# Fp32 idle matmuls, a score tile moved back and early roots behind the exponentials, at the start of an attention and MLP kernel

## The chip, the cores and the metric

One core of one Trainium2 chip. The metric is the device time of one execution in microseconds (us).

In the profile PE is TensorE (PEld its weight loads), ACT is ScalarE, DVE is VectorE, POOL is GpSimd and SP is the engine that issues most DMAs. L232 is line 232 of the kernel; the changed kernel has one line more ahead of most statements, so L231 before is L232 after.

## The reference

```python
# attention over 8 batches x 12 heads, 448 positions, 64 per head
q_n, k_n = rmsnorm(q, g_q), rmsnorm(k, g_k)
scores = (q_n @ k_n.T) / 8
attn = exp(scores - max(scores)); attn = attn / (sum(attn) + 1e-9)
x = (attn @ v)                          # to (3584, 768)
# MLP over the 3584 tokens
h = x @ w_in                            # 768 -> 2048
g = maximum(h, 0) + alpha * minimum(h, 0)
out = g @ w_out                         # 2048 -> 768
```

## The kernel before

The heads of a batch are taken in pairs, six groups a batch, 48 in all. Per group: squares of q and k (`sq`), row sums (`ss`, VectorE), the reciprocal root in two small ScalarE steps (`rr`), the scaled q and k (`qs`, GpSimd mostly), their transposes (`qT`, `kT`: for the first groups by TensorE, later by DMA, followed by a VectorE product with the gain), scores (`sc`, TensorE), the exponential (`expT`, ScalarE), the denominator (`dn`) and the values (`av`). The product of values and reciprocal denominator is `xT` (VectorE), which feeds the MLP: `hT` (TensorE), `ah` = alpha x hT (ScalarE), `gT` = max(hT, ah) (VectorE), and the output product `op` or `opa`, copied to `osb` by VectorE.

Work is written in bursts: some score tiles and their exponentials, then some MLP units to fill TensorE. In all timelines below an engine runs its own instructions in the order in which they are written. In batch 0 there is no MLP work yet; idle matmuls (`spin`) fill TensorE there.

```python
idle = gT[:, 0, :S]                      # zeros to multiply, in a row of gT
nc.vector.memset(idle, 0.0)
# ... (cut)
def begin(ft):                           # units 0 to 3 of batch 0 start before xT is whole
    if ft < 2:
        begun[ft] = bank("hT", False)
    elif ft == 2:                        # units 2 and 3: two banks of ONE tile, hTb
        t = psa.tile([128, 2, 512], FP32, name="hTb", tag="acc")
        begun[2], begun[3] = t[:, 0], t[:, 1]
    up_part(begun[ft], 0, ft, 0, G - 1)

def up(b, ft, spare=False):
    # ... (matmuls of the unit into hT)
    ah = ffn.tile([128, S], FP16, name="ah", tag="ah", bufs=3)
    nc.scalar.activation(out=ah, in_=hT[:, :S], func=AF.Copy, scale=alpha_sb[:, ft : ft + 1])
    nc.vector.tensor_max(out=gT[:, ft, ds((b & 1) * S, S)], in0=hT[:, :S], in1=ah)

def spin(count):
    if count:
        ps = psf.tile([128, 512], FP32, name="spin", tag="mm")
        for _ in range(count):
            nc.tensor.matmul(out=ps[:, :S], lhsT=ident, rhs=idle, start=True, stop=True)
# ... (cut)
spin(22)
ct = psf.tile([128, 512], FP32, name="ct", tag="mm")   # alpha and gains, transposed
nc.tensor.transpose(ct[:, : NF + 2], rows, ident32[: NF + 2, : NF + 2])
spin(6)
# ... (cut: main loop, burst n)
    if lead:                             # the burst of group 2's denominator
        begin(3)
        for t in tiles[2:]:
            score(*t)
    for t in tiles[:1] if wait else tiles[1:] if lead else first_tiles:
        soft(*t)
    # ... (cut)
    if n in roots:
        y = roots[n]
        work = [(root, (y,)), (scale, (y, "q")), (scale, (y, "k"))]
        if lead:
            late = [(3, f, a) for f, a in work]
        else:
            for f, a in work:
                f(*a)
    # ... (cut)
    if n < den_at[G - 1] - 1 and plain and n not in turns:
        spin(4)
```

## Time and profile before

| what | before |
|---|---|
| time, median of 3 runs | 435.9 us (435.75 to 436.28) |
| span of the profiled run | 434.5 us |
| PE busy / ACT / DVE / POOL | 96% / 64% / 47% / 40% |
| TensorE instructions as compiled (weight loads and matmuls) | 9986 |
| granted clock, mean | 0.995 (half for one window, 13.5 to 16.9 us) |

From 57 us on TensorE is the bound and its only large gap is one of 1.49 us ahead of 85.93, so only its gaps in the start can be won.

In the profile of the kernel before, the queue q8 (instruction) has 39 packets of 16 KB each (0.64 MB), beside 9986 TensorE instructions: one packet for 256 of them on average. The prediction and the text below call such a stretch of TensorE's instructions a block; that it is 256 long is an estimate from these two counts, and the two stalls at numbers 705 and 1729, 4 x 256 apart, agree with it.

Two further views matter for what came of it; they are not in the prediction. The first is ScalarE's timeline at the fourth `ah`, which reads the second bank of hTb. The second is VectorE's timeline at 90 us, around the DMA transpose of the k of group 7. Columns of a timeline: start, duration, engine, line, operation, output <- input, shape, count, and in brackets the idle time ahead of it and what ended it.

```profile
45.39 0.64 ACT L353 ACTIVATE ah<-hTb,cols 128x448 f16<-128x448 f32 x1
...
46.73 0.64 ACT L353 ACTIVATE ah<-hTb,cols 128x448 f16<-128x448 f32 x1 [0.24 <-DVE gT L354]
```
```profile
90.86 0.55 DVE L191 TENSOR_SCALAR kT<-kT,gain 128x896 f16<-128x896 f16 x1 [0.49 <-DMA kT<-qs]
91.73 1.09 DVE L311 TENSOR_TENSOR xT<-av,rden 128x896 f16<-128x896 f32 x1 [0.31 <-PE av L260]
92.73 2.07 DVE L153 TENSOR_REDUCE ss<-sq 128x14 f32<-128x896 f32 x2
94.72 0.55 DVE L376 COPY osb<-op 128x384 f32<-128x384 f32 x1
```

The reader is to see two waits that look harmless. The fourth `ah` waits for a `gT`, though its own hT is done; 0.24 us, because a root stood between. And VectorE goes from kT to osb almost without a gap: a delay of kT at 90.86 by more than the 0.31 us that xT still waits for av delays osb at 94.72.

### The profile page before, as it was taken

Reading aid. Unit: us, or ns where it says so; the run is one execution under the profiler, and the core shown is the slowest. Engines: PE = TensorE matmul, PEld = TensorE weight load, DVE = VectorE, ACT = ScalarE, POOL = GpSimd, SP = SyncE. Lnnn points to the kernel's source line nnn. Section 1 sums busy time; section 2 is a strip of 40 time slices with the busy share of each in tenths; the row PEclk is TensorE's granted clock in tenths of the full one; section 3 lists DMA queues with packets and bytes.
Section 4 is the critical chain, followed back from the end, with each engine's and each line's share of the span. In section 5 each row is a group of like instructions: output and inputs, shape, how many; then the busy total and the mean of one; then the engine's idle time right before and its main releaser. Section 6 shows DMA issues by size and latency. Waiting matters only on the chain.

```text
span 434.5 us, 11509 instructions
## 1 busy us (share of the span) xinstructions
PE 417.4 (96%) x4977; PEld 215.9 (50%) x4977; DVE 204.9 (47%) x304; ACT 279.4 (64%) x385; POOL 175.8 (40%) x133
## 2 busy tenths in 40 slices
PE   7888799899999999999999999999999999999996
PEld 3344344354455445544555445554555545555564
DVE  3755564544554463546454463555453354233421
ACT  4997787588877577758757577757757587132300
POOL 5799792585373626074153636174133000000000
PEclk9899999999999999999999999999999999999999
DMA  8999999999668743968076752945082300211133
GB/s 186 234 234 218 166 210 175 201 174 189 158 104 178 170 107 62 203 101 195 20 137 156 156 129 55 200 101 121 20 150 48 80 4 21 55 38 28 28 72 75
DMA packets 70387, 53.85 MB, mean 124 GB/s; under 512 B 37424, under 2 KB 70336, under 8 KB 70336
## 3 DMA queue, kind: packets, MB, share of 16 engines
q1 hardware_dynamic: 55536, 40.19, 42.8%
q0 software_dynamic: 13984, 11.81, 18.3%
q10 hardware_dynamic: 816, 1.11, 1.1%
q8 instruction: 39, 0.64, 0.6%
q14 instruction: 12, 0.10, 0.1%
HBM read 45.62 MB, written 11.01 MB: 130 GB/s over the span
## 4 chain that ended last, share of the span: by engine, by line
PE 88%; DVE 4%; ACT 4%; issue 1%; DMA 1%; SPq 0%; ACTq 0%
PE op L364 28%; PE hT L326 21%; PE hTa L326 10%; PE sc L231 8%; PE opa L364 6%; PE dn L260 5%; PE av L260 5%; ACT expT L245 3%; PE avb L260 3%; DVE ss L153 2%; DMA nat<-in_k_dram 1%; PE tps L205 1%; DVE gT L354 1%; DVE osb L376 1%; ACT ah L353 1%
## 5 line engine op out<-in xcount | busy, mean ns | idle before, releaser
L245 ACT ACTIVATE expT<-sc,expb 128x896 f16<-128x896 f32 x168 | 161.6, 1005 | 38.8 <-PE sc L231 38.1
L364 PE MATMUL op<-w_out_sb,gT 128*128 128x384 f16 (+1 forms) x752 | 126.3, 323 | 0.0
L170 POOL TENSOR_TENSOR qs<-nat,rr 128x896 f16<-128x896 f32 x44 | 76.7, 1763 | 120.0 <-ACT rr L165 89.5
L364 PEld LDWEIGHTS <-gT 128*128 128x128 f16 x912 | 85.7, 98 | 64.8 <-issue 12.2
L326 PEld LDWEIGHTS <-w_in_sb 128*128 128x128 f16 x768 | 73.2, 98 | 74.9 <-issue 10.4
L326 PE MATMUL hT<-xT,w_in_sb 128*128 128x448 f16 x510 | 107.0, 353 | 2.0 <-DVE gT L354 2.0
L147 POOL TENSOR_TENSOR sq<-nat 128x896 f32<-128x896 f32 x44 | 73.4, 1683 | 39.9 <-DMA nat<-in_q_dram 29.1
L353 ACT ACTIVATE ah<-hT,cols 128x448 f16<-128x448 f32 x85 | 53.9, 635 | 44.0 <-PE hT L326 44.0
L354 DVE TENSOR_TENSOR gT<-hT,ah 128x448 f16<-128x448 f32 x85 | 52.8, 624 | 52.7 <-ACT ah L353 52.7
L376 DVE COPY osb<-op 128x384 f32<-128x384 f32 (+1 forms) x47 | 25.8, 549 | 90.5 <-PE op L364 90.5
L231 PE MATMUL sc<-qT,kT 64*32 64x448 f16 (+1 forms) x1092 | 54.0, 357 | 6.1 <-ACT expT L245 3.4
L153 DVE TENSOR_REDUCE ss<-sq 128x14 f32<-128x896 f32 x48 | 50.5, 1078 | 7.1 <-ACT sq L145 6.2
L326 PE MATMUL hTa<-xT,w_in_sb 128*128 128x448 f16 x246 | 53.2, 352 | 0.0
L353 ACT ACTIVATE ah<-hTa,cols 128x448 f16<-128x448 f32 x41 | 26.1, 635 | 31.2 <-PE hTa L326 31.2
L354 DVE TENSOR_TENSOR gT<-hTa,ah 128x448 f16<-128x448 f32 x41 | 25.6, 624 | 26.0 <-ACT ah L353 26.0
L231 PEld LDWEIGHTS <-kT 64*32 64x32 f16 (+1 forms) x1092 | 15.2, 93 | 37.3 <-issue 32.9
L364 PE MATMUL opa<-w_out_sb,gT 128*128 128x384 f16 x160 | 27.7, 326 | 0.0
L260 PE MATMUL dn<-expT,ones 64*32 64x448 f16 (+1 forms) x812 | 24.8, 350 | 2.6 <-issue 1.7
L311 DVE TENSOR_TENSOR xT<-av,rden 128x896 f16<-128x896 f32 x16 | 17.5, 1092 | 19.1 <-PE av L260 14.7
L260 PEld LDWEIGHTS <-vt 64*32 64x32 f16 (+1 forms) x1260 | 18.9, 94 | 13.2 <-issue 2.2
L260 PE MATMUL av<-expT,vt 64*32 64x448 f16 (+1 forms) x812 | 24.1, 349 | 0.0
L260 PEld LDWEIGHTS <-ones 64*32 64x32 f16 (+1 forms) x812 | 13.0, 94 | 12.6 <-issue 6.3
(43 smaller groups left out, 162.6 us busy)
## 6 DMA issues: line engine op xcount, KB each, us to landing
out_dram<-osb SPq DMA_DIRECT2D x109, 96.0 KB, 2.3
nat<-in_q_dram SPq DMA_DIRECT2D x46, 224.0 KB, 5.6
nat<-in_k_dram SPq DMA_DIRECT2D x46, 224.0 KB, 5.7
vt<-in_v_dram POOLq DMA_DIRECT2D x16, 336.0 KB, 6.4
w_in_sb<-in_moe_w_in_dram POOLq DMA_DIRECT2D x12, 256.0 KB, 7.4
w_out_sb<-in_moe_w_out_dram POOLq DMA_DIRECT2D x4, 768.0 KB, 11.5
nat<-in_q_dram ACTq DMA_DIRECT2D x2, 224.0 KB, 4.9
nat<-in_k_dram ACTq DMA_DIRECT2D x2, 224.0 KB, 6.3
```

Of the source, the lines that this page charges most:

```text
L147: nc.gpsimd.tensor_mul(out=sqf, in0=src, in1=src)
L153: nc.vector.tensor_reduce(out=ss_t[y][:, "qk".index(nm)].rearrange("p h j -> p (h j)").unsqueeze(2), in_=sqs[y, nm], axis=AXIS_X, op=ALU.add,)
L170: eng.tensor_mul(out=t.rearrange("p j h d -> p h j d"), in0=nat[y, nm], in1=rr_t[y][:, "qk".index(nm)].unsqueeze(3).broadcast_to((128, 2, ...
L231: nc.tensor.matmul(out=sc[ds(64 * g + m * c, m), par, :S].rearrange("p (j c) -> p j c", j=J), lhsT=kT[ds(64 * par, 64), j, g, ts(c, m)], r ...
L245: nc.scalar.activation(out=expT[y][:, j], in_=scs[y, j][:, :, :S], func=AF.Exp, scale=QK_SCALE, bias=expb[:, 0:1],)
L260: nc.tensor.matmul(out=accs[g][ds(m * h, m), :S], lhsT=weights(g, y, par, ts(c, m), j), rhs=expT[y][ds(64 * g, 64), j, par, :], start=(j = ...
L311: nc.vector.tensor_mul(out=x, in0=av[:, :, :S], in1=r)
L326: nc.tensor.matmul(out=hT[:, :S], lhsT=w_in_sb[:, g * G + i, ts(ft, 128)], rhs=xT[b][:, g, i, :], start=(i == 0 and g == 0), stop=(i == G ...
L353: nc.scalar.activation(out=ah, in_=hT[:, :S], func=AF.Copy, scale=alpha_sb[:, ft : ft + 1])
L354: nc.vector.tensor_max(out=gT[:, ft, ds((b & 1) * S, S)], in0=hT[:, :S], in1=ah)
L364: nc.tensor.matmul(out=ops[c][:, :PW], lhsT=gT[:, ft, ts(t, 128)], rhs=w_out_sb[:, ft, ds(oh * OH + c * PW, PW)], start=(ft == 0), stop=(f ...
L376: nc.vector.tensor_copy(out=o[:, ts(c, PW)], in_=ops[c][:, :PW])
```

## The change

Its intent: keep TensorE's clock up with fewer and wider idle instructions, and stop ScalarE and VectorE from getting in each other's way in the first burst with MLP units. Three parts.

1. *Idle matmuls.* Mostly fp32 on bitcast zeros in place of fp16: 3 fp32 and 18 fp16 for 22 fp16 at the start, 1 fp32 for 6 after ct, 1 fp32 for 4 in five bursts. A fp32 matmul compiles to four TensorE instructions (two loads, two products: the trace of after has 18 and 18 of them for 9 fp32 matmuls), a fp16 one to two, so the program gets 24 instructions shorter on TensorE (9962).
2. *Lead burst.* Its third score tile and its exponential go behind units 2 and 3 of those begun ahead; the two row sums of group 5 go ahead of the units' gT on VectorE.
3. *Early roots.* The root and scaling of groups 4 and 5 go behind the exponentials of their burst.

```diff
-    nc.vector.memset(idle, 0.0)
+    idle32 = gT[:, 0, :].bitcast(FP32)
+    nc.vector.memset(gT[:, 0, :], 0.0)
@@ spin
+                out=ps[:, :S], lhsT=idle32[:, :128] if wide else ident,
+                rhs=idle32 if wide else idle, start=True, stop=True,
@@
-    spin(22)
+    spin(3)
+    spin(18, False)
     ct = ...
-    spin(6)
+    spin(1)
@@ main loop
-            for t in tiles[2:]:
-                score(*t)
-        for t in tiles[:1] if wait else tiles[1:] if lead else first_tiles:
+        for t in tiles[:1] if wait else tiles[1:2] if lead else first_tiles:
@@
             if lead:
-                late = [(3, f, a) for f, a in work]
+                late = [(3, score, tiles[2]), (4, soft, tiles[2])]
+            if lead or wait and y < TD:
+                late += [(late[-1][0], f, a) for f, a in work]
@@
-        if ups_first and n in dens and not lead:
+        if ups_first and n in dens:
@@
-                if n in jobs and not (lead and done < 4):
+                if n in jobs:
@@
-            spin(4)
+            spin(1)
```

More of the change, by code (lines that the diff above doesn't have):

```diff
@@ L387, in down, with spin @@
                 )
-    def spin(count):
-        if count:
-            ps = psf.tile([128, 512], FP32, name="spin", tag="mm")
-            for _ in range(count):
-                nc.tensor.matmul(
-                    out=ps[:, :S], lhsT=ident, rhs=idle, start=True, stop=True
-                )
+    def spin(count, wide=True):
+        ps = psf.tile([128, 512], FP32, name="spin", tag="mm")
+        for _ in range(count):
+            nc.tensor.matmul(
+                out=ps[:, :S], lhsT=idle32[:, :128] if wide else ident,
+                rhs=idle32 if wide else idle, start=True, stop=True,
+            )
     bursts, dens, avs, first_in, last_in = [], {}, {}, {}, {}
@@ L702 @@
                         del jobs[n]
-                if late and done == late[0][0]:
-                    for _, g, c in late:
-                        g(*c)
-                    late = []
+                while late and done == late[0][0]:
+                    _, g, c = late.pop(0)
+                    g(*c)
         if not gaps[n] and n in turns:
```

## The prediction

> **What bounds the kernel now.** I read the page first, then TensorE's waits, then the timeline of the first 100 us engine by engine, then the DMA issues and the packets of the instruction queue.
>
> ```profile
> PE 417.4 (96%) x4977; PEld 215.9 (50%) x4977; DVE 204.9 (47%) x304; ACT 279.4 (64%) x385; POOL 175.8 (40%) x133
> PE   7888799899999999999999999999999999999996
> DMA  8999999999668743968076752945082300211133
> q8 instruction: 39, 0.64, 0.6%
> ```
>
> The reader sees TensorE (PE) full from about the sixth slice (54 us) to the end, and the DMA engines full over the first ten slices. What the change can win lies in the start, and whatever TensorE wins there reaches the end only if nothing else holds it up before 100 us. TensorE's waits say how much there is:
>
> ```profile
> PE sc L231 <- ACT expT L245: 3.4, 6, 1.4
> PE hT L326 <- DVE gT L354: 2.0, 3, 0.9
> PE dn L260 <- issue: 1.7, 2, 1.5
> PE sc L231 <- issue: 1.4, 1, 1.4
> ```
>
> After the first matmul there are 11.0 us in 17 waits; these four rows are 8.5. The timeline of TensorE places the four that matter, and those of ScalarE (ACT) and VectorE (DVE) say why:
>
> ```profile
> 36.06 0.57 PE L231 MATMUL sc<-qT,kT 64*64 64x448 f16 x7 [1.37 <-issue]
> ...
> 49.60 1.29 PE L326 MATMUL hT<-xT,w_in_sb 128*128 128x448 f16 x6 [0.87 <-DVE gT L354]
> ...
> 52.63 0.38 PE L231 MATMUL sc<-qT,kT 64*64 64x448 f16 x4 [1.42 <-ACT expT L245]
> ...
> 85.93 0.95 PE L260 MATMUL dn<-expT,ones 64*64 64x448 f16 x16 [1.49 <-issue]
> ```
> ```profile
> 50.58 0.32 ACT L164 ACTIVATE rr<-ss,epsb 128x28 f32<-128x28 f32 x1 [1.79 <-DVE ss L153]
> ```
> ```profile
> 45.01 1.16 DVE L354 TENSOR_TENSOR gT<-hT,ah 128x448 f16<-128x448 f32 x2 [2.05 <-ACT ah L353]
> ...
> 47.94 1.07 DVE L153 TENSOR_REDUCE ss<-sq 128x14 f32<-128x896 f32 x1
> 48.94 0.62 DVE L354 TENSOR_TENSOR gT<-hT,ah 128x448 f16<-128x448 f32 x1
> 49.47 1.08 DVE L153 TENSOR_REDUCE ss<-sq 128x14 f32<-128x896 f32 x1
> ...
> 77.75 0.45 DVE L191 TENSOR_SCALAR kT<-kT,gain 128x896 f16<-128x896 f16 x1 [0.85 <-DMA kT<-qs]
> ```
>
> Around 50 us two row sums (ss) sit ahead of the gT products on VectorE, the root (rr) waits 1.79 us for them on ScalarE with an exponential behind it, and TensorE waits for both, although VectorE had just idled 2.05 us. The two "issue" waits have no releaser; the packets of the instruction queue explain them. One starts at 33.71 and takes 0.94 us, one starts at 83.00 and takes 1.33: TensorE goes on 1.4 and 1.6 us after each has landed. The stalled instructions are numbers 705 and 1729 of TensorE's records, 1024 apart[...].
>
> [...] No fp32 matmul of this size is in the trace. [...] granted clock 0.76 over 13 to 20 us is one such window, 13.4 to 16.8 in the clock's records, and full clock begins at 6.7 us. [...]
>
> **The change part by part.**
>
> *Fp32 idle matmuls.* 48 of fp16 become 18 of fp16 and 9 of fp32. [...] Start: the first no longer waits for the identity but for a memset twice as long (0.24 us before, about 0.47 now), so it begins at 1.5 instead of 1.37. Three cold fp32: to 6.0. Two of the 18 cold, 16 warm: to 9.75. The transpose ct moves from 8.72 to about 9.8, its copy from 9.50 to about 10.0; VectorE's next job waits for a root until 10.20 anyway. One fp32: to 10.7, and the first real transposes start at 10.74. So 0, with 0.1 us to spare. [...] There ScalarE sets the pace (7.46 busy of 8 us in 20 to 28), so a different throttled window would give nothing either.
>
> *The shift of the blocks.* I counted the instructions of the two compiled programs: 9986 and 9962 on TensorE (a fp32 matmul is four of them). Every block boundary after the idle matmuls falls 24 instructions later in the work. The one of 34.69 us moves over 7 score matmuls and 5 of hT, which are slow: 0.5 + 1.0 us. [...] of 1.37 us about 0.1 to 0.3 stays. Gain 1.1 to 1.3, and TensorE is on the chain there (28 to 43 us).
>
> *Score tile and reductions.* (Times of before, without the shift.) hT of the units begun ahead starts at 43.02 right after xT (VectorE, 42.96), no longer behind a score; the four ah run from 43.45 to 45.7 at 0.52 each, and the exponential follows to 46.5. The two ss move into VectorE's idle stretch 42.96 to 45.01 (2.07 us), so the first gT stays at 45.0. The fifth gT comes at 47.7 instead of 48.94, and hT behind it at 48.6 with no wait: -0.9 to -1.0.
>
> *Early roots.* The root of group 4 moves from 45.9 to 46.5: GpSimd's (POOL's) scaling of q and k starts 0.5 later, still in time for its transposes. The root of group 5 moves behind both exponentials: ah of the sixth unit at 48.7 instead of 51.06, the second exponential ends at 50.2 instead of 52.6, and the scores waiting for it start at 50.24 instead of 52.63: -2.4 in all, the -1.0 above included.
>
> Sum at 57 us: 1.2 + 2.4 = 3.6 us earlier.
>
> *What takes part of it back.* The first score of group 6 (79.95) needs kT by DMA transpose, landed at 77.73, behind a backlog of w_out and v that GpSimd begins to issue at 49.87. That work follows group 4's scaling, so it moves only by -1.2 + 0.5 = -0.7. kT lands near 77.0, VectorE multiplies it (0.45), then frees the accumulator with xT (1.09): opa can start at 78.7, against 80.26 before. Of 3.6 us, 1.6 are left. The second fetch stall follows[...]. I take it to shrink from 1.49 to about 0.5. Sum: 1.6 + 1.0 = 2.6; I take 0.1 off for new small waits. From 95 us TensorE has no gap of size, so 2.5 us stay to the end: 435.9 - 2.5 = 433.4.
>
> **The rivals.** (1) DMA pins the kernel harder: kT lands at 77.7 as before and the second stall stays whole. For it: the DMA row is full to 76 us. Then 0.8 is left at opa and the end is 435.1. (2) Both stalls go and kT follows TensorE. [...] Against it: group 4's scaling is later, not earlier. Then 3.6 + 1.4 = 5.0 and 430.9. (3) The start loses: if the full clock comes later than 6.7 us, ct and its copy delay the first kT by up to 0.7 us; 433.4 becomes 434.1. (4) A new block boundary falls on a fast stretch: at 325 us one nearly stalls already (0.22 us). That costs up to 1.5: 434.9.
>
> **Range and chances.** 433.4, and 431.5 to 435.3 in 8 of 10: the top is rival 1 or 4, the bottom most of rival 2. 2% is 8.7 us, and TensorE's waits of the whole execution are 11.0 us, so faster by that much is nearly impossible; slower by it would need six new stalls. Faster 0.01, same 0.985, slower 0.005.
>
> **What would show it.** The issue wait at 36 us falls from 1.37 to under 0.4 and hT comes before it; the waits for gT and expT of 0.87 and 1.42 vanish; the two ss follow xT near 42 us; tps of group 4 starts 3 us or more earlier than 52.95; kT's wait of 0.85 on VectorE grows to over 2 us; an opa waits for xT. Wrong would be: an issue wait above 1 us at a new place before 100 us, ScalarE's first exponential later than 13.7 us, or hT waiting for an xT that follows a late log.

## More of the kernel before

Score tiles, `hT`, `op` and the like lie in PSUM, in banks from which ScalarE and VectorE read them; `hTb` is one tile of two banks. The other tiles lie in SBUF.

## The result, and the profile after

| | before | after |
|---|---|---|
| time, median of 6 runs | 436.12 us (435.75 to 436.34) | 434.62 us (433.44 to 435.20) |
| span of the profiled run | 434.5 us | 432.8 us |
| ratio | | 0.9964 (0.9951 to 0.9977) |

A ratio is the mean time of one kernel's fast runs over that of the other's in the same rounds, so it is not quite the ratio of the medians. The kernel is 0.36% faster: "same" by a measure of 2%, inside the predicted range, with 1.5 us won where 2.5 were predicted.

TensorE's waits of the kernel after (us in total, times, longest):

```profile
PE sc L232 <- ACT expT L246: 3.8, 8, 1.0
...
PE hT L327 <- DVE gT L355: 1.1, 3, 0.5
...
PE hT L327 <- issue: 0.3, 1, 0.3
PE dn L261 <- issue: 0.2, 1, 0.2
```

A wait on "issue" is called a fetch stall below: the three of TensorE in the kernel before end 1.41, 1.60 and 1.44 us after a packet of the instruction queue has landed. The first shrank from 1.37 us to 0.25: in both kernels the load of the stalled matmul is number 705 of TensorE's records, and the packet started at 33.71 us (1.05 us long after, 0.94 before), but number 705 is a score before and a hT after. The second, of 1.49 us, is gone: the 0.2 of dn is another one, at 324.09 us, and the kernel before had it too (0.22 at 325.39). The waits for gT shrank from 2.0 to 1.1; the waits for expT grew from 3.4 in 6 to 3.8 in 8. TensorE's timeline places them:

```profile
36.30 0.74 PE L327 MATMUL hT<-xT,w_in_sb 128*128 128x448 f16 x3 [0.25 <-issue]
...
44.32 1.29 PE L327 MATMUL hT<-xT,w_in_sb 128*128 128x448 f16 x6 [0.53 <-DVE gT L355]
...
46.95 0.38 PE L232 MATMUL sc<-qT,kT 64*64 64x448 f16 x4 [1.02 <-ACT expT L246]
...
50.57 0.96 PE L206 MATMUL tps<-ident,qs 128*128 128x128 f16 x14
...
78.82 2.76 PE L365 MATMUL opa<-w_out_sb,gT 128*128 128x384 f16 x16 [0.61 <-DVE xT L312]
...
91.86 0.57 PE L232 MATMUL sc<-qT,kT 64*64 64x448 f16 x8 [0.50 <-DVE kT L192]
```

Set beside the same instructions of before, these give a ledger of how far TensorE was ahead:

| instruction of TensorE | before | after | ahead by |
|---|---|---|---|
| first scores | 13.03 | 12.85 | 0.18 |
| scores behind the first fetch stall | 38.18 | 36.97 | 1.21 |
| transposes of group 4 | 52.95 | 50.57 | 2.38 |
| opa | 80.26 | 78.82 | 1.44 |
| op behind the second fetch stall | 87.00 | 83.87 | 3.13 |
| scores behind it | 94.43 | 91.86 | 2.57 |
| end of the span | 434.5 | 432.8 | 1.7 |

So 3.13 us had been won by 84 us and 1.7 were left. Where were they lost? The new waits are in VectorE's timeline. First the burst, then the two transposes:

```profile
41.67 2.07 DVE L154 TENSOR_REDUCE ss<-sq 128x14 f32<-128x896 f32 x2
43.66 1.15 DVE L355 TENSOR_TENSOR gT<-hT,ah 128x448 f16<-128x448 f32 x2
44.72 0.61 DVE L355 TENSOR_TENSOR gT<-hTb,ah 128x448 f16<-128x448 f32 x1
...
77.32 0.45 DVE L192 TENSOR_SCALAR kT<-kT,gain 128x896 f16<-128x896 f16 x1 [2.81 <-DMA kT<-qs]
...
91.25 0.56 DVE L192 TENSOR_SCALAR kT<-kT,gain 128x896 f16<-128x896 f16 x1 [4.00 <-DMA kT<-qs]
91.73 1.08 DVE L312 TENSOR_TENSOR xT<-av,rden 128x896 f16<-128x896 f32 x1
92.73 2.06 DVE L154 TENSOR_REDUCE ss<-sq 128x14 f32<-128x896 f32 x2
94.72 0.54 DVE L377 COPY osb<-op 128x384 f32<-128x384 f32 x1
```

The last four rows start at 91.25, 91.73, 92.73 and 94.72; before it was 90.86, 91.73, 92.73 and 94.72. VectorE idled 4.00 us for kT of group 7, and behind that single wait its queue runs at the times of before to the hundredth. (That they are the same is chance: before, xT waited 0.31 us for av behind an earlier kT; now it follows a later kT at once.) TensorE's next hT needs the accumulator that osb frees: it waited 0.50 us for osb and began at 95.31, against 97.22 before. With this wait and the one for kT, the lead of 3.13 us has become 1.91; by 100 us it is 1.5, after one more wait of 0.15 us and smaller ones, and it is 1.7 at the end. The chain of work that ended last says what holds that kT (start, duration, what):

```profile
68.92 8.38 DMA kT<-qs
...
77.31 9.18 DMA nat<-in_k_dram
...
86.60 1.70 POOL qs L171
...
88.31 2.91 DMA kT<-qs
```

Before, the same stretch of the chain was nearly all TensorE's (scores, dn, op), with the 1.49 us stall. Now it is DMA. Its nat row is a load of group 9, though, which landed at 86.50 while GpSimd was scaling already. GpSimd's timeline shows what the scaling of group 7 followed, after and then before:

```profile
83.32 1.68 POOL L148 TENSOR_TENSOR sq<-nat 128x896 f32<-128x896 f32 x1 [1.83 <-DVE ss L154]
84.95 3.33 POOL L171 TENSOR_TENSOR qs<-nat,rr 128x896 f16<-128x896 f32 x2
```
```profile
82.32 1.68 POOL L147 TENSOR_TENSOR sq<-nat 128x896 f32<-128x896 f32 x1 [0.39 <-DMA nat<-in_k_dram]
83.95 3.34 POOL L170 TENSOR_TENSOR qs<-nat,rr 128x896 f16<-128x896 f32 x2
```

In both kernels the SP queue issues the transpose of group 6, then loads, then the transpose of group 7. In that order the k of group 8 landed at 83.16 (82.16 before), GpSimd squared it 0.16 us later, at 83.32 (82.32 before), and only then, in its own order, scaled the q and k of group 7, 1.0 us later than before. (The profile names a row sum, which ended at 83.17; before, that sum came after this square, so the square doesn't need it.) The transpose itself was quicker (2.9 against 3.5 us from issue to landing), so kT came 0.39 us later than before, though TensorE was 3 us ahead.

What put that k back was probably a packet of the instruction queue. In the kernel after, one starts at 79.51 and takes 1.34 us, and the first load that lands behind it, the second half of this k, comes 2.44 us after the load before it, where its neighbours are 1.1 us apart. Before, the packet starts at 83.00, when this k has landed, and the gap (2.45 us) falls behind the first half of the q of group 9. In 13 of the 14 traces a gap of 2.3 to 2.5 us follows that packet (not in wout_late). So in the kernel after, with TensorE ahead, the packet came 3.49 us earlier (79.51 against 83.00), and with it a load that GpSimd waits for landed 1.0 us later (83.16 against 82.16). No run tests this by itself.

And ScalarE in the burst:

```profile
43.52 0.63 ACT L354 ACTIVATE ah<-hTb,cols 128x448 f16<-128x448 f32 x1
45.36 0.63 ACT L354 ACTIVATE ah<-hTb,cols 128x448 f16<-128x448 f32 x1 [1.22 <-DVE gT L355]
45.90 1.00 ACT L246 ACTIVATE expT<-sc,expb 128x896 f16<-128x896 f32 x1
```

The fourth `ah` now waits 1.22 us for the gT of unit 2, which ended at 45.33 behind the two row sums and two other gT. The exponential follows it, and the scores at 46.95 wait 1.02 us for that.

### The profile page after: what moved, and what is told of

Its sections match the earlier page's. It is cut to its first block, busy times and chain, and to the rows that moved or that the text cites.

```text
span 432.8 us, 11487 instructions
## 1 busy us (share of the span) xinstructions
PE 418.0 (97%) x4965; PEld 216.8 (50%) x4965; DVE 204.3 (47%) x304; ACT 278.6 (64%) x385; POOL 175.6 (41%) x133
## 3 DMA queue, kind: packets, MB, share of 16 engines
q0 software_dynamic: 13984, 11.81, 18.1%
## 4 chain that ended last, share of the span: by engine, by line
PE 81%; ACT 5%; DMA 5%; DVE 4%; POOL 2%; issue 1%; DVEq 0%; POOLq 0%
PE op L365 26%; PE hT L327 20%; PE hTa L327 10%; PE sc L232 7%; PE opa L365 6%; PE dn L261 4%; PE av L261 4%; ACT expT L246 3%; DMA kT<-qs 3%; PE spin L394 2%; DMA nat<-in_k_dram 2%; PE avb L261 2%; DVE ss L154 2%; POOL qs L171 1%; DVE gT L355 1%
## 5 line engine op out<-in xcount | busy, mean ns | idle before, releaser
L148 POOL TENSOR_TENSOR sq<-nat 128x896 f32<-128x896 f32 x44 | 73.4, 1681 | 40.5 <-DMA nat<-in_q_dram 36.6
L355 DVE TENSOR_TENSOR gT<-hT,ah 128x448 f16<-128x448 f32 x85 | 52.8, 623 | 49.7 <-ACT ah L354 49.6
L278 ACT ACTIVATE rden<-dn 128x896 f32<-128x896 f32 x16 | 14.5, 907 | 7.3 <-PE dn L261 7.3
```

Source lines behind the costliest of these rows:

```text
L148: nc.gpsimd.tensor_mul(out=sqf, in0=src, in1=src)
```

## The experiments

Four questions: which part of the change earns its 1.5 us; whether the fetch stall is a matter of where blocks of instructions begin; what holds the fourth `ah`; and whether the clock or the DMA takes the rest back. Every kernel gave the right result. A column gives in how many runs the mean granted clock was 0.996 or less; one half-rate window of 3.41 us, as in the kernel before (13.50 to 16.91), takes 0.004 from the mean over 435 us. Kernels of one job ran on the same chip beside the kernel before.

| kernel | job | median us (range) | ratio to before (95%) | runs with clock of 0.996 or less |
|---|---|---|---|---|
| before | 1 | 435.93 (435.16 to 440.56) | | 5 of 11 |
| fp32_only | 1 | 434.60 (433.62 to 435.93) | 0.9962 (0.9928 to 0.9996) | 0 of 6 |
| bursts_only | 1 | 436.38 (435.74 to 438.30) | 1.0009 (0.9974 to 1.0045) | 3 of 6 |
| shift_only | 1 | 435.57 (434.91 to 438.45) | 0.9997 (0.9957 to 1.0036) | 4 of 6 |
| shift_undone | 1 | 436.77 (435.21 to 438.54) | 1.0003 (0.9964 to 1.0042) | 2 of 6 |
| before | 2 | 436.40 (435.52 to 440.30) | | 6 of 11 |
| ah_fourth | 2 | 435.37 (433.96 to 437.11) | 0.9950 (0.9914 to 0.9986) | 1 of 6 |
| sums_back | 2 | 434.18 (433.50 to 436.00) | 0.9939 (0.9905 to 0.9974) | 0 of 6 |
| ct_early | 2 | 435.40 (434.40 to 436.97) | 0.9960 (0.9925 to 0.9996) | 4 of 6 |
| wout_late | 2 | 438.22 (434.76 to 439.99) | 1.0016 (0.9971 to 1.0061) | 5 of 6 |
| before | 3 | 436.75 (435.52 to 440.30) | | 6 of 10 |
| pair_first | 3 | 433.75 (431.85 to 434.81) | 0.9915 (0.9876 to 0.9954) | 0 of 6 |
| start_fp32 | 3 | 436.71 (435.26 to 440.03) | 0.9999 (0.9957 to 1.0042) | 5 of 6 |
| both | 3 | 435.80 (434.18 to 440.07) | 0.9984 (0.9936 to 1.0033) | 5 of 6 |
| after_again (the kernel after) | 3 | 434.61 (434.04 to 436.93) | 0.9951 (0.9916 to 0.9987) | 1 of 6 |

Jobs 2 and 3 shared the chip and some of the runs of before.

### fp32_only: part 1 alone

The kernel before with the idle matmuls of the kernel after and nothing else.

```diff
-    spin(22)
+    spin(3)
+    spin(18, False)
     ct = ...
-    spin(6)
+    spin(1)
@@
-            spin(4)
+            spin(1)
```

> Only the fp32 idle matmuls (and the longer memset); bursts as before. Theory 1 (instruction blocks): the wait without releaser near 36 us falls from 1.37 to about 0.25 us and the one near 85 us shrinks or goes, so 0.8 to 1.8 us faster than before (434.3 to 435.3). Theory 2 (clock): the half-rate window at 13.4 to 16.8 us is gone and that is what brings the gain; same time, but the exponentials between 13 and 30 us would then have to run closer together than before (ScalarE's first sixteen end by over 0.5 us earlier, counted from the first). Theory 3: the gain is all in the bursts, and this one stays at 436.1.

Measured: 434.60 us, 0.9962. TensorE's timeline:

```profile
52.02 0.38 PE L232 MATMUL sc<-qT,kT 64*64 64x448 f16 x4 [1.41 <-ACT expT L246]
...
85.39 0.38 PE L261 MATMUL dn<-expT,ones 64*64 64x448 f16 x4 [0.99 <-issue]
```

The first fetch stall fell to 0.47 us (at 36.91); the wait for the exponential is 1.41 as before (1.42), so the bursts are untouched. The ratio is that of the whole change. What parts 2 and 3 add to it is within the noise. In this trace TensorE's lead over before is 0.6 us from the first stall to opa, 1.1 behind the second stall, which is still 0.99 here, and 1.7 at the end; the last step is at 325 us, where the kernel before waits 0.22 us on "issue" and this one doesn't.

### bursts_only: parts 2 and 3 alone

The kernel after with the fp16 idle matmuls and the counts of before.

```diff
-    spin(3)
-    spin(18, False)
+    spin(22)
     ct = ...
-    spin(1)
+    spin(6)
@@
-            spin(1)
+            spin(4)
```

> Only the score tile, the reductions and the roots; fp16 idle matmuls as before, so the instruction blocks lie as before. Theory 1: the wait of 1.4 us near 35 us stays; TensorE is about 1.2 us earlier at 57 us; the kT that lands near 77.5 us takes most of it back, and a fetch stall of 0.5 to 1.5 us near 84 us stays. 0.2 to 1.0 us faster than before (435.1 to 435.9). Theory 3: the whole gain of the change, 434.6.

Measured: 436.38 us, 1.0009: nothing. The trace says why:

```profile
35.56 0.57 PE L231 MATMUL sc<-qT,kT 64*64 64x448 f16 x7 [1.04 <-issue]
...
79.32 0.38 PE L231 MATMUL sc<-qT,kT 64*64 64x448 f16 x4 [0.98 <-DVE kT L191]
80.32 2.76 PE L364 MATMUL opa<-w_out_sb,gT 128*128 128x384 f16 x16 [0.61 <-DVE xT L311]
```

The first fetch stall is back in the same place (the scores), with 1.04 us of the 1.37. The bursts did win time: the transposes of group 4 began at 51.28 against 52.95. But kT of group 6 landed at 78.79, later than in the kernel before (77.73), and opa at 80.32 stands where it stood before (80.26). What TensorE wins in the bursts it waits for at the transpose. The second fetch stall, which I had expected to stay, is gone, and op behind it begins at 85.37 (87.00 before). But kT of group 7 lands at 92.58 (90.83 before) and osb at 94.72 moves to 96.09, so that the profiled run ends 0.5 us ahead of before.

### shift_only: 24 instructions fewer, no fp32

```diff
-    spin(22)
+    spin(20)
@@
-            spin(4)
+            spin(2)
```
(in the kernel before: 12 fp16 idle matmuls less, two instructions each)

> The kernel before with 12 fewer fp16 idle matmuls (2 in place of 4 in five bursts, 20 in place of 22 at the start): 24 TensorE instructions fewer, so the blocks lie as in the changed kernel, with no fp32 at all. Theory 1: within 0.5 us of the run with the fp32 idle matmuls alone, the wait near 36 us at about 0.25. Theory 2 (clock or fp32 itself): no gain, 436.1, the half-rate window stays or grows.

Measured: 435.57 us, 0.9997 (0.9957 to 1.0036). The fetch stall near 36 us was gone from the list of waits, so with 24 instructions fewer, and no fp32, it goes: from 1.37 us to none. Four of the six runs took 434.91 to 435.58; two took 437.71 and 438.45. The profiled one is the 438.45: its clock was half from 15.5 to 29.1 us and again from 83.7 to 87.1, and opa took 4.44 us in place of 2.77. With fewer idle matmuls the blocks moved but the clock fell (0.996 or less in four of six runs). Part 1 does the first without the second (none of six in fp32_only).

### shift_undone: the fp32 idle matmuls, but blocks where they were

The kernel after with 12 one-column matmuls added in the bursts, two instructions each.

```diff
+    def tiny(count):
+        ps = psf.tile([128, 512], FP32, name="tiny", tag="mm")
+        for _ in range(count):
+            nc.tensor.matmul(out=ps[:, :1], lhsT=ident, rhs=idle[:, :1], start=True, stop=True)
@@
             spin(1)
+            tiny({0: 2, 1: 2, 3: 2, 4: 3, 6: 3}[n])
```

> The changed kernel with 12 matmuls of one column added in the bursts where TensorE waits anyway: the blocks lie as before the change, all else as changed. Theory 1: a wait without releaser of 1.2 to 1.5 us is back near 34.5 us, and one near 82 to 84 us; about 1 us slower than the changed kernel (435.2 to 436.0), near the run with the bursts alone. Theory 2: as the changed kernel, 434.6, full clock from 13 to 20 us.

Measured: 436.77 us, 1.0003; the gain is gone, and the stall is back at the same scores as before:

```profile
36.66 0.96 PE L232 MATMUL sc<-qT,kT 64*64 64x448 f16 x7 [1.86 <-issue]
```

The clock was half from 36.6 to 40.0 us, a window that follows the stall, so this row took 0.96 us and not 0.57. Together with shift_only this settles the first stall: it goes by the place in the order of TensorE's instructions, and 24 of them move it (1.37 us before, none in shift_only, 1.86 here). The second stall is another matter: I had expected it back at 82 to 84 us, and it is gone here and in bursts_only, where the blocks lie as before, while 0.99 us of it stayed in fp32_only, where they are moved. In the two without it TensorE had waited for kT of group 6 and xT (1.0 and 1.6 us) just ahead, which may have given the packet time to land; that is argued and not tested.

### ah_fourth: is it the ring of three `ah` buffers?

A first theory for the wait of 1.22 us: `ah` has three buffers, so the fourth must wait for the first gT. The fourth `ah` gets a place of its own, in a part of w_out that isn't loaded yet.

```diff
-        ah = ffn.tile([128, S], FP16, name="ah", tag="ah", bufs=3)
+        if (b, ft) == (0, 3):
+            ah = w_out_sb[:, NF - 1, :S]
+        else:
+            ah = ffn.tile([128, S], FP16, name="ah", tag="ah", bufs=3)
```

> The changed kernel, with the fourth ah (unit 3 of batch 0) in a place of its own instead of in the ring of three. Theory A (ring): ScalarE's fourth ah waited 1.22 us for a gT that the two row sums had pushed back; that wait goes, the scores' wait of 1.02 us near 47 us goes, and the transposes of group 4 start at 49.2 to 49.8 instead of 50.57. Theory B (the kT of group 6 pins the kernel): kT still lands at 76.3 to 77.5, opa waits for xT, and the time stays within 0.6 us of the changed kernel (434.0 to 435.0). Rival: no pin, 433.4 or less.

Measured: 435.37 us, and the wait stayed to the hundredth:

```profile
46.44 0.63 ACT L357 ACTIVATE w_out_sb<-hTb,cols 128x448 f16<-128x448 f32 x1 [1.22 <-DVE gT L358]
```

The theory fell.

### sums_back: the row sums where they were

```diff
-        if ups_first and n in dens:
+        if ups_first and n in dens and not lead:
@@
-                if n in jobs:
+                if n in jobs and not (lead and done < 4):
```

> The changed kernel with the two row sums of group 5 back behind the fourth and fifth unit, as before the change; score tile and roots as changed. Theory A: the fourth ah waits under 0.3 us, but the sums then hold the fifth gT and the root again; TensorE at 57 us within 0.6 us of the changed kernel, and by theory B the end the same within 0.5 us (434.1 to 435.1). Rival: the place of the sums is what carries the bursts' part; then TensorE is over 1 us later at 57 us.

Measured: 434.18 us, 0.9939; within the noise of the kernel after. The fourth `ah` waits 0.69 us in place of 1.22, so the sums ahead of the gT make up 0.53 of that wait; 0.69 has another cause. Loads and the first stall shift the bursts of a run as a whole, so I count from the scores behind the first fetch stall to the transposes of group 4: 14.77 us in the kernel before (38.18 to 52.95), 13.60 in the kernel after (36.97 to 50.57), 13.08 here (37.63 to 50.71). So the score tile and the roots win 1.69 us there, and the move of the row sums loses 0.52 of it. It isn't saved later: the scores 7.53 us behind those transposes (58.24, in the kernel after 58.10) are equally far in both. The sums didn't hold the fifth gT either, as theory A had it; that one waited for its `ah`.

### pair_first: both `ah` of hTb ahead of both gT

What is left: units 2 and 3 are two banks of one PSUM tile, and the program lets the `ah` of unit 3 (ScalarE) wait until the gT of unit 2 (VectorE) has read that tile. If both `ah` are written first, ScalarE has not to wait for VectorE between them.

```diff
+        if (b, ft) == (0, 3):
+            return
+        fts = (2, 3) if (b, ft) == (0, 2) else (ft,)
+        hTs = [begun[n] if b == 0 and n in begun else hT for n in fts]
+        ahs = []
+        for n, h in zip(fts, hTs):
             ah = ffn.tile([128, S], FP16, name="ah", tag="ah", bufs=3)
+            # the activation, from h of unit n
+            ahs.append(ah)
+        for n, h, ah in zip(fts, hTs, ahs):
+            # the max, into gT of unit n
```

> The changed kernel, with both ah of the two units that share one PSUM tile (hTb) ahead of both their gT. The ring theory fell: with a place of its own the fourth ah waited 1.22 us as before. Theory A2: it waits for the gT of the unit in the same PSUM tile (VectorE's read of the tile, then ScalarE's). Then the fourth ah starts within 0.3 us of the first gT's end instead of 1.1 us after it, the scores' wait of 1.02 us near 47 us falls under 0.3, and the transposes of group 4 start about 1 us earlier counted from the first gT. Theory B: kT of group 6 takes it back, time within 0.6 us of the changed kernel on this chip. Rival: the wait stays as it was, and has yet another cause.

Measured: 433.75 us (431.85 to 434.81), 0.9915: the best kernel of all. The fourth `ah` and the exponential behind it:

```profile
45.18 0.63 ACT L360 ACTIVATE ah<-hTb,cols 128x448 f16<-128x448 f32 x1 [0.15 <-DVE gT L363]
45.72 1.00 ACT L246 ACTIVATE expT<-sc,expb 128x896 f16<-128x896 f32 x1
```

The wait is 0.15 us, until the first gT is done (45.1), which frees the first of three `ah` buffers; and the gT of unit 2, which now comes behind that `ah`, waits in its turn for it to end. The scores' wait of 1.02 us at 46.95 is gone. This run had begun the first scores later (13.37 against 12.85) and kept 0.61 us of fetch stall, and yet its transposes of group 4 began at 50.39, before those of the kernel after (50.57). Counted as above the bursts take 12.54 us (from 37.85), 1.06 less than in the kernel after. So the order of these two reads held the fourth `ah`, and with the buffers ruled out the shared tile is what is left to tie them; a kernel with two tiles was not run. In the profiled run the gain is lost again at the transposes: kT of group 6 landed at 77.36, opa began at 78.89, kT of group 7 kept VectorE waiting 3.96 us, and the span is 432.8 as in the kernel after. Two other runs were much faster (431.85 and 432.25). No trace shows what was different in them.

### wout_late: less traffic ahead of the transpose

The second half of w_out is issued two bursts later, in the kernel after.

```diff
-        after(first + c // 2 * 2, load_w_out, c)
+        after(first + c // 2 * 4, load_w_out, c)
```

> The changed kernel with the second half of w_out issued two bursts later, behind the scaling of group 6, so that kT's transposes go ahead of 1.5 MB. Theory B: kT of group 6 lands at 71 to 73 instead of 77.3, VectorE's wait of 2.8 us and opa's of 0.6 go, TensorE is about 1.4 us earlier at opa (77.4). What follows is open: the loads of group 8 and w_out itself now come later; if the op of the second half (83.9) waits for w_out or the kT of group 7 lands after 92, the gain is lost: 433.2 to 435.5. Rival: kT lands no earlier.

Measured: 438.22 us, with a wide range. kT of group 6 did come earlier, at 75.58 (77.30 in the kernel after), and opa began at 78.26 with no wait at all. Most of that is not the backlog: the transpose was issued at 67.51 in place of 68.92, because GpSimd no longer issues that half of w_out ahead of the scaling, and took 8.06 us in place of 8.38. The w_out load now goes out at 67.43, right ahead of it; only the transpose of q before both got shorter (4.72 us in place of 9.19). So this run doesn't show how long kT would take without the backlog. And the load that was moved is then missing:

```profile
87.28 2.40 PE L365 MATMUL op<-w_out_sb,gT 128*128 128x384 f16 x8 [2.48 <-DMA w_out_sb<-in_moe_w_out_dram]
```

The clock was half from 87.6 to 91.1 us after it. Put off in this way, the traffic only changed who waited.

### ct_early: is the start too long?

In the kernel after, ct begins at 9.98 us (8.72 before) and VectorE waited for its copy. Here 14 fp16 idle matmuls stand in place of 18, with four one-column matmuls later so that blocks begin where they did.

```diff
-    spin(18, False)
+    spin(14, False)
@@
             spin(1)
+            tiny({0: 1, 1: 0, 3: 1, 4: 1, 6: 1}[n])
```

> The changed kernel with four fp16 idle matmuls fewer ahead of ct, and four matmuls of one column in the bursts so that the instruction blocks stay where they are. Theory C (ct holds the start): VectorE's scaling of the first k waited 0.5 us for the copy of ct; that goes, the first exponential comes 0.3 to 0.5 us earlier measured from the landing of the first k, and the end 0.2 to 0.5 us earlier (434.1 to 434.4). Rival: the idle matmuls taken away let the clock fall in a window after 13 us: slower.

Measured: 435.40 us, 0.9960. ct began at 8.82 and VectorE no longer waited for it, but the clock was half from 11.3 to 18.1 us, and the first transposes took 1.88 us in place of 1.08. The first scores began 5.88 us after the first square of k, in the kernel after 5.65. No gain.

### start_fp32 and both: all of the start in fp32

Six fp32 idle matmuls and no fp16 at the start, which makes the program another 24 instructions shorter; `both` has pair_first's edit too.

```diff
-    spin(3)
-    spin(18, False)
+    spin(6)
```

> The changed kernel with 3 more fp32 idle matmuls in place of the 18 of fp16 at the start: 24 TensorE instructions fewer again, so the block that still stalls 0.25 us near 36 us begins two or three denominators later, where TensorE waits for an exponential anyway. Theory 1: no wait without releaser over 0.15 us before 80 us, 0.2 to 0.6 us faster than the changed kernel on this chip; ct moves to about 9.2 and VectorE's wait for it goes. Rival: less idle work at the start lets the clock fall to half in a window between 10 and 20 us, and this shows as slower.

> Both edits together, as the candidate that may beat the changed kernel. If nothing pins the first 100 us: 1.2 to 1.6 us faster than the changed kernel on this chip. By theory B: 0.3 to 0.8 us, with a longer wait of VectorE for kT near 77 us (over 3.5 us).

Measured: 436.71 and 435.80 us. There was no fetch stall before 80 us, so the shift worked once more; but the clock was half from 11.8 to 18.6 us in one and 11.7 to 18.5 in the other. The columns of this line of start_fp32 are the stretch, its length, busy time and number of instructions of each engine, granted clock, DMA share and GB/s:

```profile
10.00:20.00 10.00, 8.01 (x56) 3.33 (x56) 5.41 (x7) 7.88 (x12) 7.21 (x6) 0.66 1.16 237
```

The stall had been 0.25 us in the kernel after; the profiled span of start_fp32, with a granted clock of 0.66 in this stretch, is 434.1 us against 432.8.

### after_again: the kernel after, once more, for its spread

No edit.

> The changed kernel once more, beside the other three on one chip and for a second trace. 434.3 to 435.4; if TensorE's waits near 80 us add up to over 1.5 us in this trace, a window at half clock follows and the run is over 1 us longer than the shortest.

Measured: 434.61 us, with five runs of 434.04 to 434.85 and one of 436.93, which happens to be the profiled one. Its kT of group 6 landed at 80.03 in place of 77.30:

```profile
80.56 0.38 PE L232 MATMUL sc<-qT,kT 64*64 64x448 f16 x4 [2.75 <-DVE kT L192]
81.56 4.44 PE L365 MATMUL opa<-w_out_sb,gT 128*128 128x384 f16 x16 [0.61 <-DVE xT L312]
```

As expected, the two waits, over 1.5 us together, are followed by a half-rate window (82.2 to 85.6): opa took 4.44 us in place of 2.76. The late transpose cost twice here, by the wait and by the slow window after it. This is the one run from the slow tail of the kernel after that has a trace. That of the kernel before has low clocks too, but I have no trace of one of its slow runs.

## Why the prediction was right or wrong

**The total** was right: 434.62 us in a range of 431.5 to 435.3, the class "same" as given. The gain was 1.5 where 2.5 were predicted. The attribution was not right: within the noise part 1 alone earns the whole gain, and the bursts, which the prediction gave 2.4 of 3.6 us at 57 us, earn nothing by themselves that shows in the time (0.9974 to 1.0045): most of what they win by 51 us is gone at the end. And the number at opa came out (1.44 us ahead, 1.6 predicted) although the bursts had won 1.2 less than predicted, because kT and not TensorE sets opa.

**The first fetch stall** was right in place and size: 0.1 to 0.3 us were to stay, 0.25 stayed, five hT instructions stand before it, and the gain is 1.21, or 1.03 without the 0.18 that was there at the first scores already (predicted 1.1 to 1.3). That the packet itself would hardly move was the author's estimate, not shown by the trace of before; it started at 33.71 us in both kernels and landed at 34.76 in place of 34.65. Moving the block back by 24 instructions brought the stall back (shift_undone); moving it without fp32 took it away (shift_only).

**The start** was right in its result, 0, and off in a term. The 0.18 us of the ledger are not the change's: the first q had landed earlier, and its square began at 5.31 (5.50 before). The first scores follow the first square of q by 7.5 us in both, and that of k by 5.65 us (5.51 before). What a fp32 idle matmul takes no trace had shown; the prediction's 4.5 us for three cold ones (1.5 to 6.0) were the estimate. Measured, they took 4.85 us, and a warm one 1.02 us, where the four of fp16 that it replaces took 0.93.

**The clock** was named in one clause: a different throttled window would give nothing. For the window of 13.5 to 16.9 us (13.4 to 16.8 in the prediction) this is right. The kernel after hasn't got it, and its ScalarE-bound stretch runs 0.2 us earlier throughout, which is the 0.18 of the start and no more. But the prediction had no place for runs in which the clock falls. Five of eleven runs of the kernel before in job 1 were at 0.996 or less, none of fp32_only's. Mean of the other runs alone: 435.61 (6 runs) against 434.70 (6), so about 0.9 us; of all runs: 436.25 against 434.70, so 1.55. By this split, about two fifths of part 1's gain in that job are fewer half-rate windows. It is a rough split of few runs.

**The bursts** were mis-sized: predicted 2.4 us, measured 2.38 - 1.21 = 1.17. The step that failed is "the four ah run from 43.45 to 45.7 at 0.52 each". The fourth waited 1.22 us, for the gT of the unit that shares its PSUM tile; pair_first takes the wait away, ah_fourth rules out the buffers. In the profile of before this wait was there, with 0.24 us, and I read past it. "The first gT stays at 45.0", with the sums in VectorE's idle time, comes out, but that time was no longer idle: with the first `ah` earlier, the first gT could have followed it by 0.66 us, as in sums_back, and behind the sums it came 1.28 us later (42.38 to 43.66). So the move of the sums, which was to win, lost: 0.53 of the 1.22 us, and 0.52 us at the transposes.

**GpSimd's scaling** was to begin so that w_out is issued 0.7 us earlier. It was issued at 50.73 against 49.87, 0.86 later, because the root of group 4 sat behind that delayed exponential.

**The first pin by DMA** was right: kT was to land near 77.0 and opa to start at 78.7; they did at 77.30 and 78.82, with the predicted wait of opa for xT (0.61) and VectorE's wait grown to 2.81. The size is partly luck: the transpose was issued 0.85 us later than before and took 1.3 us less (8.38 against 9.66).

**The second stall** was to shrink to 0.5, by the estimate of when its packet would come, which the trace of before doesn't show, and is gone: the packet landed at 80.85 us, and TensorE came to the same number of its records, 1729, at 83.21 (before: landed at 84.33, and on at 85.93). TensorE was 3.13 us ahead behind it, against a predicted 2.6.

**What failed** is the last sentence of the sum: "From 95 us TensorE has no gap of size, so 2.5 us stay to the end", with 0.1 off for new small waits. There was a second pin, kT of group 7 at 91.22, in the four microseconds that the sum skips; the queue of VectorE carried it to osb at 94.72. It took 3.13 - 1.91 = 1.2 of the 3.13 - 1.7 = 1.4 us that went. I had checked the transposes of group 6 against the faster TensorE and not those of group 7, although the same SP queue serves both. The other traces bear it out: in the ten with the changed bursts and w_out in its place, kT of group 7 lands between 91.22 and 94.78 us, and the span ends 341.2 to 342.0 us after it in each.

**The rivals.** Rival 1 (DMA pins harder) was the nearest in kind, but with another transpose than it named; its second half, that the second stall stays, is wrong. Rival 2 needed the transpose to follow TensorE; it didn't. Rival 3 is wrong for the kernel after, and right in kind for ct_early and start_fp32, where the clock fell after a shorter start. No new stall of rival 4 came.

**What stays open.** Why kT of group 6 lands anywhere from 77.10 to 80.03 us in the runs of fp32_only, the kernel after and its repetition. How much of part 1 is blocks and how much is clock, beyond the split above: shift_only has the blocks and loses clock. And what pair_first's two fastest runs did.

## What to carry to other kernels

When an early engine is freed, don't stop at the first DMA that holds it: check each later load and transpose that one queue serves, for its landing time is a limit of its own, and an engine with a fixed order carries that limit to work that has nothing to do with it (here VectorE, from kT at 91.22 us to osb at 94.72). A change of a few instructions won or lost a microsecond here by the place of a stall in TensorE's order (24 instructions: 1.37 us of stall, 0.25 or 1.86) and by whether the clock held (opa in 2.76 us, or 4.44 at half rate); test both by themselves before crediting a reordering. Idle time of before is not idle time of after: the row sums went into a gap that the change itself closed. And where a program orders the reads of one PSUM tile by two engines, write them so that neither has to wait for the other (the fourth `ah` waited 1.22 us, and 0.15 once both `ah` came first).

## What the runs show of instruction packets, the clock, fp32 and the two-bank tile

- Instruction packets: with 39 of them in the kernel before, TensorE had three waits on "issue" of 0.2 us or more (1.37, 1.49 and 0.22 us), with two in the kernel after (0.25 and 0.23). The two long ones fell where the DMA engines were full (DMA share 1.23 from 33.70 to 36.06 us and 1.06 from 82.00 to 85.93); the one in shift_undone was 1.86 us. In the kernel before TensorE goes on 1.41 and 1.60 us after the packet has landed. Number 1473 of TensorE's records, 256 ahead of the second stalled one, began at 77.32 us; the packet started 5.7 us later, at 83.00.
- The clock: half rate came behind windows in which TensorE waited only in part. Count windows of 3.41 us from a change of rate in the clock's records (in the kernel before it was full from 6.67 us for 6.83 us and then half for 3.41). The waits of TensorE that lie in the window ahead of a half-rate one sum to 1.7 us in the kernel before (10.1 to 13.5) and start_fp32, 1.8 in shift_undone, 2.0 in ah_fourth, 2.35 in after_again and 2.5 in wout_late, and to 1.6 ahead of the first one in shift_only; windows with 1.4 (before, at 36 us), 1.55 (sums_back, at 79 us) and 1.8 (shift_only, 49.6 to 53.0) stayed at full rate. So in these runs every window at full rate with over 1.9 us of waiting was followed by half rate, none with under 1.6, and between the two it went both ways. When full rate comes back they don't show: shift_only stayed at half for four windows, with waits of 0.6 us at most in the first three.
- fp32: a product of 128x128 with 128x448 in fp32 took 1.02 us warm and 1.62 cold (three in 4.85), in two loads and two products; the fp16 one took 0.19 warm and 0.37 cold.
- The two-bank tile: in this kernel the program's wait covers a tile of two banks, so `ah` of the one bank waited 1.22 us for `gT` of the other. No run here tried the two reads at once.
